# Attention batches on a plan of 25 FFN groups, held outputs of five tiles stored by SyncE, and five more query chunks transposed by DMA

## The chip, the cores and the metric

The kernel runs on 1 core of one Trainium2 chip. The metric is the device time of one execution in microseconds (us). The profile is of one execution and counts its span, some 2 us shorter than that time. A run is called slow here when it is over 1.5% above the fastest of the same kernel. The granted clock is the share of TensorE's full clock that the profile shows as granted (1.000 is full); the DMA share is the time that packets took, as a share of the time of the core's 16 DMA engines (it can exceed 1). PSUM is the memory that matmuls write to, and a PSUM tile has to be emptied before it is used again.

## The reference, cut to what matters

```python
def _attn_ref(q, k, v):                        # (8, 8, 576, 64): batch, heads, rows, head size
    q_p = phi(q, cos_w, sin_w)                 # relu(x)*cos, relu(x)*sin side by side: 128 features
    k_p = phi(k, cos_w, sin_w)
    kv = np.einsum('bhsf,bhsd->bhfd', k_p, v)
    z = np.sum(k_p, axis=2)
    num = np.einsum('bhsf,bhfd->bhsd', q_p, kv)
    den = np.einsum('bhsf,bhf->bhs', q_p, z)[..., None] + 1e-06
    return num / den
def _moe_ref(x, w1, w2, w3, w_out):            # x: the attention output as 4608 rows of 512
    return ((x @ w1) * (x @ w2) @ w3) @ w_out
```

There are 8 batches of attention, each of five chunks of rows, and 9 tiles of 512 rows for the feed-forward part (FFN). Both share TensorE.

Of the kernel before, what the change touches and what calls it, by code (L numbers as in the profile page):

```python
# [10 lines left out]
FP32 = mybir.dt.float32  # L11
# [5 lines left out]
P = 128  # L17
H, S, D = 8, 576, 64
F = 2 * D
NCH = 5  # L20
# [48 lines left out]
def kernel(  # L69
# [128 lines left out]
    def other_loads(behind):  # L198

        seen = sm.tile([P, 1], BF16, name="seen", bufs=1)  # L200
        nc.gpsimd.tensor_copy(out=seen[:], in_=behind)
        nc.gpsimd.dma_start(out=w2b[:, :, ds(512, 256)], in_=w2v[:, :, ds(512, 256)])
        load_w12(768, 256)
        nc.gpsimd.dma_start(out=woutb[:], in_=moe_w_out.rearrange("(c p) m -> p c m", p=P))
        for jp in range(8):
            load_w3(jp)
            if jp == 4:
                load(1, "k")
        load(1, "qv")
        load(2, "kqv")  # L210


    w3Ts = {}
# [22 lines left out]
    def order_of(b):  # L236

        return [0, 1, 2, 3, 4] if b % 2 == 0 else [4, 0, 1, 2, 3]

    def dma_q(b):  # L240

        return order_of(b)[5 if b < 2 else 2 if b == 2 else 0:]

    feat = {}

# [201 lines left out]

    def open_held():
        wst_stack.close()
        held_pool.append(ctx.enter_context(tc.tile_pool(name="held", bufs=8)))  # L450

    def store_held():
        osb, g = held.pop(0)
        store(nc.gpsimd, osb[:, :, :], g, 2)

    def ffn_groups(t):
        x = xT[t]
# [47 lines left out]
        for ms in range(3 if t == NT - 1 else 4):  # L505
            ops = ffn_tile()
            for jc in range(8):
                nc.tensor.matmul(ops[:, :], lhsT=abT[:, jc, ts(ms, 128)], rhs=w34b[:, jc, :],  # L508
                                 start=(jc == 0), stop=(jc == 7))
                if jc == 3:  # L510
                    yield
            if ms % 2 == 0:
                if 1 <= t <= 4:
                    osb = held_pool[0].tile([P, 2, 512], FP32, name="held")
                else:
                    pool = (fsb, held_pool[0])[ms // 2]
                    osb = pool.tile([P, 2, 512], FP32, name="osb", bufs=1)
            nc.scalar.copy(out=osb[:, ms % 2, :], in_=ops[:, :])  # L518
            if t == NT - 1:
                store((nc.sync, nc.scalar)[ms % 2], osb[:, ms % 2:ms % 2 + 1, :], 4 * t + ms, 1)  # L520
            elif ms % 2 == 1 and 1 <= t <= 4:
                held.append((osb, 4 * t + ms - 1))
            elif ms % 2 == 1:
                store(nc.gpsimd, osb[:, :, :], 4 * t + ms - 1, 2)
            yield
        if t == NT - 1:
            for at, n, eng in ((0, 256, nc.scalar), (256, 128, nc.sync), (384, 128, nc.scalar)):
# [10 lines left out]
    def prep_units(b, parts=(prep_k, prep_q, prep_v)):  # L538
        return [(lambda f=f, c=c: f(b, c)) for f in parts for c in order_of(b)]

    def load_piece(b, i, dst, c):

        seen = sm.tile([P, 1], BF16, name="seen", bufs=1)
        nc.gpsimd.tensor_copy(out=seen[0:ROWS[c], :], in_=dst[0:ROWS[c], c, 0, 0:1])  # L544
        load(b, "kqv"[i // 2], i % 2)

    def interleaved(b, pieces=range(5)):

        units = []
        for i, c in enumerate(order_of(b)):  # L550
            units.append(lambda c=c: prep_k(b, c))
            if b + 1 < B:
                units.append(lambda c=c, i=i: load_piece(b + 1, pieces[i], feat[b][0], c))
            units.append(lambda c=c: prep_q(b, c))
            if b + 1 < B and i == NCH - 1 and pieces[i] < 5:
                units.append(lambda c=c: load_piece(b + 1, 5, feat[b][1], c))
            units.append(lambda c=c: prep_v(b, c))
        return units

    def spread(units, first, last, slots):  # L560
        for i, u in enumerate(units):
# [30 lines left out]
    for i in range(2):  # L592
        ps_ffn.append(ctx.enter_context(tc.tile_pool(name=f"ps_ffn{len(ps_ffn)}", bufs=2,
                                                     space=bass.MemoryType.PSUM)))

    for t in range(NT):
        slots = [[] for _ in range(24)]
        if t == 0:
            slots[1].append(lambda: x_tr(0, 1, by_vector=True))
            slots[1].append(lambda: q_tr(0, 3, evac=False)[1]())  # L600
            slots[1].append(lambda: num(0, 2))
            slots[3].append(lambda: num(0, 3))
            slots[3].append(lambda: x_tr(0, 2))
            slots[5].append(lambda: x_tr(0, 3))
            slots[6].append(lambda: prep_q(0, 4))
            slots[11].append(lambda: feature_buffers(1))
            slots[8].append(lambda: q_tr(0, 4))
            slots[10].append(lambda: num(0, 4))
            slots[12].append(lambda: x_tr(0, 4))
            slots[14].append(lambda: w3_tr(0))  # L610
            between = [[] for _ in range(32)]
            later = [[] for _ in range(24)]
            spread(prep_units(1, (prep_k,)), 6, 8, between)
            spread(prep_units(1, (prep_q,)), 10, 12, between)
            spread(prep_units(1, (prep_v,)), 13, 13, between)
            attention_at(1, between, kv=(14, 14, 14, 14, 15), tr=(12, 13, 17, 18, 19),
                         nu=(16, 17, 18, 20, 22), xt=(18, 19, 20, 22, 25))
            later[:8] = between[24:32]
            for jp in range(8):
                for part in range(2):  # L620
                    if part == 0 and jp < 7:
                        slots[15].append(lambda jp=jp: w3_tr(jp + 1))
                    slots[15].append(lambda jp=jp, part=part: w34_mm(jp, part))
                    slots[15] += between[2 * jp + part]
            for g in range(16, 24):
                slots[g] += between[g]
            slots[16].append(open_held)
            slots[16].append(lambda: load(3, "kqv"))
            spread(prep_units(2, (prep_k,)), 20, 23, slots)
        elif t == 1:  # L630
            for g in range(24):
                slots[g] += later[g]
            spread(prep_units(2, (prep_q,)), 0, 4, slots)
            spread(prep_units(2, (prep_v,)), 0, 4, slots)
            attention_at(2, slots, kv=(2, 3, 4, 5, 6), tr=(3, 5, 7, 9, 11),
                         nu=(8, 10, 12, 14, 16), xt=(8, 10, 12, 14, 16))
            slots[4].append(lambda: load_piece(4, 0, feat[2][1], 3))
            spread(interleaved(3, range(1, 6)), 6, 23, slots)
        else:
            if t + 1 < B:  # L640
                attention_at(t + 1, slots, kv=(0, 1, 2, 3, 4), tr=(2, 4, 7, 10, 13),
                             nu=(6, 8, 10, 12, 14), xt=(6, 8, 10, 12, 14))
            for g in {5: (3, 9, 15, 20), 6: (1, 6, 11, 16)}.get(t, ()):
                slots[g].append(store_held)
            if t + 2 < B:
                spread(interleaved(t + 2), 0, 22, slots)
        for g, _ in enumerate(ffn_groups(t)):
            for u in slots[g]:
                u()
# [30 lines left out]
```

## The kernel before: the parts that the change and the argument touch

One tile of FFN is a sequence of 24 groups of four 512-column matmuls. Attention work ("units") is put behind these groups by hand. For one batch the units are: features of keys and queries (half on ScalarE, half on VectorE), the value copy on GpSimd, the key-value product `kv_chunk`, the query transpose to `qpT`, the numerator `num` with its normalization on VectorE, and the transpose of the result block to `xT`, which the FFN tile reads.

```python
    def load(b, which, part=None):              # GpSimd's DMA; one batch is six pieces
        ...                                     # k, q, v, each in part 0 (320 KB) and part 1 (256 KB); batch 7: 512 and 64 KB
    def prep_q(b, c):
        features(b, feat_of(b)[1], raw[b, "q"], c)          # ScalarE and VectorE
        if c in dma_q(b):                                   # else by TensorE (line 326) and VectorE
            nc.sync.dma_start_transpose(out=att_of(b)["qpT"][:, :, ds(columns_of(b, c), R)],
                                        in_=feat[b][1][:R, c].rearrange("p h f -> p (h f)"))
    def dma_q(b):
        return order_of(b)[5 if b < 2 else 2 if b == 2 else 0:]
    ...
    def load_piece(b, i, dst, c):               # the copy to `seen` holds the load back until dst is there
        seen = sm.tile([P, 1], BF16, name="seen", bufs=1)
        nc.gpsimd.tensor_copy(out=seen[0:ROWS[c], :], in_=dst[0:ROWS[c], c, 0, 0:1])
        load(b, "kqv"[i // 2], i % 2)
    def interleaved(b, pieces=range(5)):        # features of batch b, and between them the loads of b + 1
        ...
```

In the steady state the features of batch t + 2 are computed during tile t, and between them the pieces of batch t + 3 are loaded. GpSimd stores most outputs; those of tiles 1 to 4 are held and leave in tiles 5 and 6.

## Time and profile before

| | before |
|---|---|
| median of the three runs (us) | 251.34 |
| span of the profiled run (us) | 249.5 |
| TensorE busy (us) | 242.9 |
| TensorE's wait for anything between 24 and 240 us | none listed |
| mean granted clock | 1.000 |

The prediction shows the lines that carry this. Two further views are needed. The first is the list of issues of single transfers (queue, count, and the median us from issue to landing):

```profile
qpT<-qp SPq DMA_TRANSPOSE x28, 6.2
xT<-xblk SPq DMA_TRANSPOSE x30, 5.4
```

The second is the order in time (start, duration, engine, line, what, and the idle time before it). Parts of it are shown below.

```profile
99.66 0.68 POOL L130 DMA_DIRECT2D qs<-in_q_dram  x1 [0.33 <-issue]
...
104.20 0.68 POOL L134 DMA_DIRECT2D qs<-in_q_dram  x1 [0.27 <-issue]
...
114.93 0.72 ACT L267 ACTIVATE qp<-qs,sinv 64x512 bf16<-64x512 bf16 x1
```

### The profile page before, as it was taken

Reading aid. Unit: us, or ns where it says so; the run is one execution under the profiler, and the core shown is the slowest. Engines: PE = TensorE matmul, PEld = TensorE weight load, DVE = VectorE, ACT = ScalarE, POOL = GpSimd, SP = SyncE. Lnnn points to the kernel's source line nnn. Section 1 sums busy time; section 2 is a strip of 40 time slices with the busy share of each in tenths; the row PEclk is TensorE's granted clock in tenths of the full one; section 3 lists DMA queues with packets and bytes.
Section 4 is the critical chain, followed back from the end, with each engine's and each line's share of the span. In section 5 each row is a group of like instructions: output and inputs, shape, how many; then the busy total and the mean of one; then the engine's idle time right before and its main releaser. Section 6 shows DMA issues by size and latency. Waiting matters only on the chain.

```text
span 249.5 us, 4973 instructions
## 1 busy us (share of the span) xinstructions
PE 242.9 (97%) x1879; PEld 130.2 (52%) x1879; DVE 141.6 (57%) x338; ACT 124.5 (50%) x209; POOL 90.9 (36%) x171
## 2 busy tenths in 40 slices
PE   8899999999999999999999999999999999999994
PEld 3478555666555455545545554555455544444443
DVE  7876665657889628905980695189227704312321
ACT  2676325925966656555655555555432242323320
POOL 7754254540533612441433326280365040023000
PEclk9999999999999999999999999999999999999999
DMA  6999999999999999999999989999798992014013
GB/s 191 183 194 199 209 204 205 198 199 198 267 133 172 170 202 158 156 181 125 160 107 206 189 100 191 190 184 159 107 203 254 240 146 65 3 32 137 1 44 127
DMA packets 80760, 39.85 MB, mean 160 GB/s; under 512 B 48224, under 2 KB 77280, under 8 KB 80736
## 3 DMA queue, kind: packets, MB, share of 16 engines
q0 software_dynamic: 37024, 27.20, 72.0%
q1 hardware_dynamic: 43280, 11.87, 31.9%
q10 hardware_dynamic: 432, 0.46, 0.5%
q8 instruction: 15, 0.25, 0.4%
q14 instruction: 9, 0.07, 0.1%
HBM read 38.80 MB, written 9.44 MB: 193 GB/s over the span
## 4 chain that ended last, share of the span: by engine, by line
PE 92%; DMA 3%; DVE 1%; issue 1%; POOL 1%; ACT 0%; POOLq 0%
PE ffnps L462 50%; PE ffnps L508 24%; PE ffnps L230 6%; PE pnum L353 4%; PE pnum L295 4%; DMA qs<-in_q_dram 3%; PE pst L326 2%; PE pst L218 1%; PE pst L390 1%; PE ffnps L531 1%; POOL vs L112 0%; DVE xblk L363 0%; PE pfirst L353 0%; ACT xT L392 0%; DVE qp L263 0%
## 5 line engine op out<-in xcount | busy, mean ns | idle before, releaser
L503 DVE TENSOR_TENSOR abT<-asb,ffnps 128x512 bf16<-128x512 bf16 x68 | 46.5, 683 | 71.4 <-PE ffnps L462 70.6
L462 PE MATMUL ffnps<-xT,w1b 128*128 128x512 bf16 (+2 forms) x320 | 74.9, 357 | 0.4 <-ACT xT L392 0.2
L462 PE MATMUL ffnps<-xT,w2b 128*128 128x512 bf16 (+2 forms) x320 | 74.9, 357 | 0.0
L499 ACT CAST asb<-ffnps 128x512 bf16<-128x512 f32 x68 | 39.8, 586 | 61.6 <-PE ffnps L462 56.0
L508 PE MATMUL ffnps<-w34b,abT 128*128 128x512 bf16 x280 | 63.0, 379 | 0.0
L462 PEld LDWEIGHTS <-w1b 128*128 128x128 bf16 x320 | 29.4, 98 | 29.6 <-issue 0.6
L508 PEld LDWEIGHTS <-abT 128*128 128x128 bf16 x280 | 26.9, 98 | 31.1
L462 PEld LDWEIGHTS <-w2b 128*128 128x128 bf16 x320 | 26.8, 98 | 20.3
L267 ACT ACTIVATE qp<-qs,sinv 128x512 bf16<-128x512 bf16 (+2 forms) x40 | 28.3, 717 | 1.6 <-DMA qs<-in_q_dram 1.6
L363 DVE TENSOR_TENSOR xblk<-pnum,den 128x512 bf16<-128x512 f32 (+1 forms) x39 | 26.9, 691 | 1.4
L436 POOL DMA_DIRECT2D out_dram<-osb x20 | 10.6, 535 | 46.0 <-ACT osb L518 46.0
L287 POOL COPY va<-vs 128x512 bf16<-128x512 bf16 (+1 forms) x30 | 18.4, 624 | 18.7 <-PE pnum L295 8.9
L267 ACT ACTIVATE kp<-ks,sinv 128x512 bf16<-128x512 bf16 (+1 forms) x35 | 24.7, 721 | 0.0
L518 ACT COPY osb<-ffnps 128x512 f32<-128x512 f32 x19 | 11.1, 585 | 21.9 <-PE ffnps L508 21.9
L353 PEld LDWEIGHTS <-qpT 128*128 128x128 bf16 x320 | 15.1, 98 | 8.6 <-DVE qpT L340 0.6
L263 DVE TENSOR_SCALAR qp<-qs,cosv 128x512 bf16<-128x512 bf16 (+1 forms) x40 | 16.5, 418 | 0.7 <-DMA qs<-in_q_dram 0.6
L295 PEld LDWEIGHTS <-kp 128*128 128x128 bf16 x280 | 13.1, 98 | 7.1
L518 ACT COPY held<-ffnps 128x512 f32<-128x512 f32 x16 | 9.4, 586 | 14.3 <-PE ffnps L508 14.3
L353 PE MATMUL pnum<-kvs,qpT 128*128 128x65 bf16 x312 | 16.5, 194 | 0.0
L544 POOL COPY seen<-kp 128x1 bf16<-128x1 bf16 (+1 forms) x20 | 3.8, 188 | 33.9 <-DVE kp L263 26.1
L230 PE MATMUL ffnps<-woutb,w3T 128*128 128x512 bf16 x64 | 15.4, 379 | 0.0
L295 PE MATMUL pnum<-va,kp 128*128 128x65 bf16 x280 | 14.1, 193 | 0.0
(88 smaller groups left out, 195.3 us busy)
## 6 DMA issues: line engine op xcount, KB each, us to landing
out_dram<-held POOLq DMA_DIRECT2D x10, 256.0 KB, 6.3
qs<-in_q_dram POOLq DMA_DIRECT2D x8, 256.0 KB, 7.9
w3b<-in_moe_w_dram POOLq DMA_DIRECT2D x8, 256.0 KB, 12.8
ks<-in_k_dram POOLq DMA_DIRECT2D x6, 320.0 KB, 10.9
qs<-in_q_dram POOLq DMA_DIRECT2D x6, 320.0 KB, 8.6
vs<-in_v_dram POOLq DMA_DIRECT2D x6, 320.0 KB, 9.0
ks<-in_k_dram POOLq DMA_DIRECT2D x6, 256.0 KB, 8.2
vs<-in_v_dram POOLq DMA_DIRECT2D x6, 256.0 KB, 10.9
```

Of the source, the lines that this page charges most:

```text
L230: nc.tensor.matmul(acc[:, :], lhsT=w3T[:, lc, :], rhs=woutb[:, lc, :], start=(lc == 0), stop=(lc == 7))
L263: nc.vector.tensor_scalar(out=dst[:R, c, :, 0:D], in0=src[:R, :, c, :], scalar1=0.0, scalar2=cosv[:R, at:at + 1], op0=ALU.max, op1=ALU.mult)
L267: nc.scalar.activation(out=dst[:R, c, 0:n, D:F], in_=src[:R, 0:n, c, :], func=ACTF.Relu, scale=sinv[:R, at:at + 1], bias=0.0)
L287: eng.tensor_copy(out=feat_of(b)[2][:R, c, :, 0:D], in_=raw[b, "v"][:R, :, c, :])
L295: nc.tensor.matmul(kvt[:, h // 4, ds((h % 4) * 65, 65)], lhsT=kp[:, c, h, :], rhs=va[:, c, h, 0:D + 1], start=(i == 0 and h % 4 == 0), sto ...
L353: nc.tensor.matmul(nt[:, h // 4, ds((h % 4) * 65, 65)], lhsT=qpT[:, h, ds(at, 128)], rhs=kvs[:, h, :], start=True, stop=True)
L363: nc.vector.tensor_tensor(out=xblk[rows], in0=n4[:, :, :, 0:D], in1=den[rows].unsqueeze(3).to_broadcast([R, 2, 4, D]), op=ALU.mult)
L462: nc.tensor.matmul(out, lhsT=w[:, kc, ts(jc, 128)], rhs=x[:, kc, tok], start=(kc == 0), stop=(kc == 3))
L499: nc.scalar.copy(out=asb[:], in_=aT[:, :])
L503: nc.vector.tensor_mul(out=abT[:, jc, :], in0=asb[:], in1=bT[:, :])
L508: nc.tensor.matmul(ops[:, :], lhsT=abT[:, jc, ts(ms, 128)], rhs=w34b[:, jc, :], start=(jc == 0), stop=(jc == 7))
L518: nc.scalar.copy(out=osb[:, ms % 2, :], in_=ops[:, :])
```

## The change

Its intent: take five more query transposes off TensorE, which is full, and make room on the DMA engines for it. The room is to come from spreading each batch evenly over 25 groups, with one load piece at a time between its steps, and from holding the first outputs until the loads are done. The core of the diff (cuts marked):

```diff
-        return order_of(b)[5 if b < 2 else 2 if b == 2 else 0:]
+        return order_of(b)[5 if b == 0 else 2 if b == 1 else 0:]
...
-        held_pool.append(ctx.enter_context(tc.tile_pool(name="held", bufs=8)))
+        held_pool.append(ctx.enter_context(tc.tile_pool(name="held", bufs=10)))
...
-        store(nc.gpsimd, osb[:, :, :], g, 2)
+        store(nc.sync, osb[:, :, :], g, 2)
...
+    def plan_batch(b):
+        z = 28 + 25 * (b - 2)
+        for i, c in enumerate(order_of(b)):
+            plan[z - 8 + 3 * i // 2].append(lambda c=c: prep_k(b, c))
+            if i == 0 and b > 2:
+                plan[z - 8].append(lambda: behind_k(b, 0, b, "q", 1))
+            plan[z - 5 + i].append(lambda c=c: prep_v(b, c))
+            plan[z - 2 + 2 * i].append(lambda c=c: prep_q(b, c))
+            plan[z + 1 + i].append(lambda c=c, i=i: kv_chunk(b, c, i))
+            plan[z + 8 + 2 * i].append(lambda c=c: num(b, c))
+            if b + 1 < B and i > 0:
+                plan[z + 8 + 2 * i].append(
+                    lambda i=i: behind_x(b, i, b + 1, "kvvq"[i - 1], (1, 0, 1, 0)[i - 1]))
+            plan[z + 8 + 2 * i].append(lambda c=c: x_tr(b, c))
+        if b + 1 < B:
+            plan[z + 7].append(lambda: behind_q(b, 4, b + 1, "k", 0))
...
+    for b in range(2, B):
+        plan_batch(b)
+    for g in (122, 124, 148, 150, *(170 + 5 * i // 2 for i in range(12))):
+        plan[g].append(store_held)
...   (batches 1 and 2 at the start are placed anew in the same manner;
...    `interleaved`, `load_piece` and the stores by GpSimd go)
```

`behind_k`, `behind_q` and `behind_x` copy one element of a key feature, a query feature or a normalized block on GpSimd and then issue the load.

More of the change, by code (lines that the diff above doesn't have):

```diff
@@ L209, in other_loads @@
         load(1, "qv")
-        load(2, "kqv")
     w3Ts = {}
@@ L512, in ffn_groups @@
             if ms % 2 == 0:
-                if 1 <= t <= 4:
-                    osb = held_pool[0].tile([P, 2, 512], FP32, name="held")
-                else:
-                    pool = (fsb, held_pool[0])[ms // 2]
-                    osb = pool.tile([P, 2, 512], FP32, name="osb", bufs=1)
+                osb = held_pool[0].tile([P, 2, 512], FP32, name="held")
             nc.scalar.copy(out=osb[:, ms % 2, :], in_=ops[:, :])
@@ L520, in ffn_groups @@
                 store((nc.sync, nc.scalar)[ms % 2], osb[:, ms % 2:ms % 2 + 1, :], 4 * t + ms, 1)
-            elif ms % 2 == 1 and 1 <= t <= 4:
+            elif ms % 2 == 1:
                 held.append((osb, 4 * t + ms - 1))
-            elif ms % 2 == 1:
-                store(nc.gpsimd, osb[:, :, :], 4 * t + ms - 1, 2)
             yield
@@ L539, in prep_units, with load_behind, behind_k, behind_q @@
         return [(lambda f=f, c=c: f(b, c)) for f in parts for c in order_of(b)]
-    def load_piece(b, i, dst, c):
+    def load_behind(ap, b, name, part):
         seen = sm.tile([P, 1], BF16, name="seen", bufs=1)
-        nc.gpsimd.tensor_copy(out=seen[0:ROWS[c], :], in_=dst[0:ROWS[c], c, 0, 0:1])
-        load(b, "kqv"[i // 2], i % 2)
-    def interleaved(b, pieces=range(5)):
-        units = []
-        for i, c in enumerate(order_of(b)):
-            units.append(lambda c=c: prep_k(b, c))
-            if b + 1 < B:
-                units.append(lambda c=c, i=i: load_piece(b + 1, pieces[i], feat[b][0], c))
-            units.append(lambda c=c: prep_q(b, c))
-            if b + 1 < B and i == NCH - 1 and pieces[i] < 5:
-                units.append(lambda c=c: load_piece(b + 1, 5, feat[b][1], c))
-            units.append(lambda c=c: prep_v(b, c))
-        return units
+        nc.gpsimd.tensor_copy(out=seen[0:64, :], in_=ap)
+        load(b, name, part)
+    def behind_k(b, i, *what):
+        load_behind(feat[b][0][0:64, order_of(b)[i], 0, 0:1], *what)
+    def behind_q(b, i, *what):
+        load_behind(feat[b][1][0:64, order_of(b)[i], 0, 0:1], *what)
+    def behind_x(b, i, *what):
+        c = order_of(b)[i]
+        r = out_rows(b, c).start
+        load_behind(att[b]["x"][c][r:r + 64, 0, 0, 0:1], *what)
+    plan = [[] for _ in range(24 * NT)]
+    def plan_batch(b):
+        z = 28 + 25 * (b - 2)
+        for i, c in enumerate(order_of(b)):
+            plan[z - 8 + 3 * i // 2].append(lambda c=c: prep_k(b, c))
[11 more added lines that the diff above has]
+            plan[z + 7].append(lambda: behind_q(b, 4, b + 1, "k", 0))
     def spread(units, first, last, slots):
@@ L611 @@
             between = [[] for _ in range(32)]
-            later = [[] for _ in range(24)]
             spread(prep_units(1, (prep_k,)), 6, 8, between)
@@ L616 @@
             attention_at(1, between, kv=(14, 14, 14, 14, 15), tr=(12, 13, 17, 18, 19),
-                         nu=(16, 17, 18, 20, 22), xt=(18, 19, 20, 22, 25))
-            later[:8] = between[24:32]
+                         nu=(16, 17, 19, 21, 25), xt=(18, 19, 21, 22, 27))
+            later = between[24:32]
+            for i in range(2):
+                between[11 + i].append(lambda i=i: behind_q(1, 2 + 2 * i, 2, "k", i))
+            between[12].append(lambda: load(2, "v", 0))
+            for i, g in enumerate((16, 17, 19)):
+                between[g].append(lambda i=i: behind_x(1, i, 2, "vqq"[i], (1, 0, 1)[i]))
             for jp in range(8):
@@ L627 @@
             slots[16].append(open_held)
-            slots[16].append(lambda: load(3, "kqv"))
-            spread(prep_units(2, (prep_k,)), 20, 23, slots)
         elif t == 1:
-            for g in range(24):
-                slots[g] += later[g]
-            spread(prep_units(2, (prep_q,)), 0, 4, slots)
-            spread(prep_units(2, (prep_v,)), 0, 4, slots)
-            attention_at(2, slots, kv=(2, 3, 4, 5, 6), tr=(3, 5, 7, 9, 11),
-                         nu=(8, 10, 12, 14, 16), xt=(8, 10, 12, 14, 16))
-            slots[4].append(lambda: load_piece(4, 0, feat[2][1], 3))
-            spread(interleaved(3, range(1, 6)), 6, 23, slots)
-        else:
-            if t + 1 < B:
-                attention_at(t + 1, slots, kv=(0, 1, 2, 3, 4), tr=(2, 4, 7, 10, 13),
-                             nu=(6, 8, 10, 12, 14), xt=(6, 8, 10, 12, 14))
-            for g in {5: (3, 9, 15, 20), 6: (1, 6, 11, 16)}.get(t, ()):
-                slots[g].append(store_held)
-            if t + 2 < B:
-                spread(interleaved(t + 2), 0, 22, slots)
+            for g, units in enumerate(later):
+                slots[g] += units
+        for g in range(24):
+            slots[g] += plan[24 * t + g]
         for g, _ in enumerate(ffn_groups(t)):
```

## The prediction

> **What bounds the kernel now.** I read the page of the profile first, then the busy time by stages, then the waits of TensorE, then the chain of waits, and last the single transfers. The share of busy time and the row of slices come from the page:
>
> ```profile
> PE 242.9 (97%) x1879; PEld 130.2 (52%) x1879; DVE 141.6 (57%) x338; ACT 124.5 (50%) x209; POOL 90.9 (36%) x171
> PE   8899999999999999999999999999999999999994
> PEclk9999999999999999999999999999999999999999
> DMA  6999999999999999999999989999798992014013
> ```
>
> TensorE is busy in 97% of the span at full granted clock, and the others in 57% or less. The digits do not tell a full engine from one with small gaps, so I asked for the busy time in three stretches (us: TensorE first, then weight loads, VectorE, ScalarE, GpSimd, the clock, the DMA share and GB/s):
>
> ```profile
> 24.00:60.00 36.00, 35.96 (x327) 21.52 (x325) 23.38 (x53) 16.64 (x30) 14.70 (x22) 1.00 1.30 203
> 60.00:200.00 140.00, 140.00 (x1094) 72.86 (x1093) 89.04 (x213) 79.33 (x133) 54.13 (x108) 1.00 1.21 176
> 200.00:244.00 44.00, 44.00 (x206) 19.92 (x205) 11.00 (x16) 14.65 (x25) 6.34 (x12) 1.00 0.27 59
> ```
>
> The reader is to see that from 24 to 244 us TensorE lacks 0.04 us in 220. Asked for the waits of TensorE in that stretch, the profile lists none; over the whole span its longest are 1.2 us at the start and 0.9 us for the first values. Busy matmul time alone can hide a slow pitch, so the chain of waits has to say what one instruction costs. From its list in order of time (start, us, what):
>
> ```profile
> by line: PE ffnps L462 49.9%; PE ffnps L508 24.2%; PE ffnps L230 5.5%; PE pnum L353 4.1%; PE pnum L295 3.6%; DMA qs<-in_q_dram 3.2%; PE pst L326 1.6%; PE pst L218 1.4%; PE pst L390 0.9%; issue 0.8%; PE ffnps L531 0.7%; POOL vs L112 0.4%; DV
> ...
> 48.09 0.45 PE pst L326 x8
> 48.53 0.86 PE ffnps L230 x4
> 49.40 0.45 PE pst L326 x8
> ...
> 69.38 0.86 PE ffnps L462 x4
> 70.25 0.45 PE pst L326 x8
> 70.69 0.26 PE pnum L295 x8
> ```
>
> Four matmuls of 512 columns take 0.86 us (216 ns each), eight of 65 columns 0.26 us, eight transposes of one query chunk 0.45 us (56 ns each), and each piece begins where the one before ended. So every transpose of line 326 lies on the path that sets the end, and VectorE, ScalarE, GpSimd and the transfers do not, as long as they deliver in time. They also deliver with difficulty: the DMA share is over 1 until 200 us.
>
> **What the Trainium skill says.** "TensorE: Matmul & The Clock Gate", section "Wait — 56ns, not 53.3ns?", gives 56 ns as the gap between matmuls of 128 columns; the 0.45 us for eight here agree. Its "Part 4: PE-mode transpose" tells of about 275 ns for one transpose in a kernel; the trace shows 219 ns as the modelled length of one, but a pitch of 56 ns, and the pitch is what is saved. "DMA: Bandwidth & Descriptors", section "Queues, rings and completion order", says that each DMA engine alternates between the queues it has work for, packet by packet: a transpose on SyncE's queue and a load on GpSimd's slow each other. The trace agrees: a transpose of a result block (xT) landed in 2.4 us at 175 us, where nothing else moved, and in 6.3 us at 99 us beside a query load. "Issuing engines are not separate DMA queues" on the same page says that another issuing engine only saves issue time; so I expect nothing of SyncE storing in place of GpSimd, beyond freeing GpSimd.
>
> **The change part by part.**
>
> Five query chunks leave TensorE: three of batch 1 (its last three) and two of batch 2 (its first two). The instruction order of the changed kernel has 80 fewer rows on TensorE, 40 weight loads and 40 transposes, and nothing else less. 5 x 0.45 = 2.23 us, all on the path. Their five copies on VectorE (0.68 us each, 3.4 us) go too, off the path. In exchange there are 33 query transposes by DMA in place of 28. One lands in 3.2 to 11.3 us (median 6.2); its use lies 10 groups later in the plan, of 0.86 us each, plus attention matmuls, some 10 us. That should hide.
>
> The outputs of tiles 0 to 4 are kept (10 buffers), two stores of 512 KB leave at groups 122 and 124, two at 148 and 150, and 12 from 170 to 197, all by SyncE. Before, tile 0 stored at 59 and 64 us, amid loads. That removes 1 MB from a crowded stretch. At the end, 12 x 0.5 MB = 6.3 MB within 28 groups (about 24 us) needs 260 GB/s. From 188 to 190 us the trace shows stores at 0.3 to 0.4 MB in a us, so they are done near group 200, before the last tile's first store at group 209. The last stores, 2 to 2.6 us to landing, are unchanged. Cost on the path: 0.
>
> Batches from 2 on follow a plan of 25 groups. The loads are no longer issued a batch ahead: pieces go out at groups 7, 10, 12, 14, 16 and 17 of the plan for features from group 17 on. The first key piece has 10 groups, the second 7 (some 6.8 us with three num steps of 0.26), the last query piece 6. Pieces landed in 4.2 to 6.9 us where they were alone and in 11 to 12 where three were issued together. A late piece stops ScalarE and VectorE, but TensorE has four PSUM tiles and can run about two groups on, so a delay under some 1.7 us costs nothing. I put 0.2 us on the path for all of it.
>
> The close call is xT. Its transpose must land before the next tile's first matmul, and the plan leaves less room than before. For batch 3 the last block that tile 3 needs is normalized behind group 65, and tile 3 starts at group 72: six groups and three num steps, 6 x 0.864 + 3 x 0.26 = 5.96 us. In the trace before, the xT transpose is issued 1.6 us after such a num step begins (118.46 to 120.08 us). So it has to land within 4.3 us. By the same sum tile 5 leaves 4.6 us, tile 7 4.6 us (no loads are left there), tiles 2, 4 and 6 about 5.2 to 5.5 us. Before, with ten query transposes and loads between them, the median was 5.4 us; where one load piece alone was near I read 3.3, 4.0, 5.2 and 6.3 us. In the plan query transposes no longer lie between the xT ones, and I take 4.5 us: nothing at tiles 2, 4, 6 and 7 most of the time, 0.2 us at tile 3 on this figure, and up to 1 us at tiles 3 and 5 if the load of the same step gets in first. I put 0.4 us for these boundaries. There is no buffer in front of them: what is late here is lost in full.
>
> Sum: 251.34 - 2.23 + 0.2 + 0.4 = 249.7 us.
>
> **The rivals.**
>
> (a) Everything hides: 251.34 - 2.23 = 249.1 us. For it: TensorE waits for nothing in the middle now, although DMA is crowded, and the plan spreads transfers. I can't get below that by more than noise, because no other TensorE row goes.
>
> (b) The wait for xT takes the place of the transposes: if each transpose lands at the 5.4 us of before, tile 3 loses 1.1, tile 5 0.8, tile 2 0.2 us: 2.1 us together, and the time is 251.2, the same as before. For it: the DMA share over 1, and each xT step sends a load piece at the same moment. Against it: the stores and the query transposes have left this stretch.
>
> (c) The loads come late: six pieces, 1.7 MB as written, want 8.6 us of DMA at the 0.2 MB per us of the trace, and with 0.7 MB of xT transposes they fill the 10 groups in which they are issued. If key or query pieces land in 9 us or more for each of six batches, ScalarE stops for 2 to 3 us each time, of which about 1 us reaches TensorE: 255 us. For it: the median key piece took 10.9 us before. Against it: those were issued early, several behind one another. The most exposed is batch 2, whose last query piece is issued behind group 19 of tile 0, near 60 us, and is wanted behind group 26, near 65 us.
>
> (d) SyncE gets too full: a DMA transpose held its queue for 1.2 us in the median and 3.9 at most; ten per batch at 2 us each are 20 us of about 24. The stores sit between the batches, where nothing waits behind them. I expect no loss.
>
> **Range and chances.** The floor is 249.1 us less some noise (the three runs of before span 0.3 us), so 248.9. Above, (b) alone gives 251.2 and a bit of (c) more: 251.8. Faster by over 2% would need 246.3 us, which no part provides: 0.01. Slower by over 2% (256.4) needs (c) in full: 0.04. Within 2%: 0.95.
>
> **What would show it.** In the changed profile, line 326's successor should have 48 transposes on TensorE instead of 88, and TensorE should still be full from 24 to 242 us but for short holes. The waits of TensorE should name a DMA of xT, if anything, at the starts of tiles 3 and 5, for 0 to 1 us. Query transposes should never be named. ScalarE should show waits for loads of keys or queries of up to 1.5 us that do not appear in TensorE's list. The number is wrong if TensorE waits at every tile start, if a feature step stops for over 2 us, or if the last stores queue behind held ones and the end behind the last matmul grows beyond the present 3.6 us.

## The result, and the profile after

The changed kernel took 274.59 us (median of 4 runs, 270.77 to 277.35), against 251.3 us. The ratio is 1.0836 (95% interval 1.0726 to 1.0946): 8.4% slower. Ratios in this document use fast runs alone, so they are not quite the ratios of the medians of all runs. Of the changed kernel two runs are fast, 273.98 and 270.77 us; where another kernel's time is compared with the changed one below, it is with their mean, 272.4 us. The four runs had mean granted clocks of 0.967, 0.967, 0.979 and 0.973; the profiled one (273.98 us) counts as fast. From the page of the changed kernel:

```profile
span 272.1 us, 4904 instructions
PE 250.1 (92%) x1839; PEld 130.1 (48%) x1839; DVE 139.0 (51%) x333; ACT 123.1 (45%) x209; POOL 70.1 (26%) x140
PE   8899999999999899599998899959995699999994
PEclk9999999999999999989999799968999799999999
DMA  8999999995799989998899579975999444888803
```

TensorE has 40 matmuls less, as planned (1839 for 1879), and yet it was busy 7.2 us more, and idle 22.0 us instead of 6.6. The digits show holes about once in a batch, and the granted clock dips at or behind most of them. The row of the DMA share dips too, to 5 and 7 where it was 9, so the DMA engines have idle time now. The waits of TensorE (us in total, times, longest):

```profile
PE ffnps L461 <- ACT asb L498: 8.0, 3, 4.9
PE ffnps L461 <- DVE abT L502: 3.4, 1, 3.4
PE ffnps L461 <- DMA xT<-xblk: 3.3, 2, 2.8
```

The first two rows, 11.4 us, name ScalarE and VectorE, which empty TensorE's PSUM tiles. What these two waited for, first ScalarE in the kernel before, then both in the changed kernel:

```profile
ACT qp L267 <- DMA qs<-in_q_dram: 1.6, 2, 1.5
```

```profile
ACT qp L266 <- DMA qs<-in_q_dram: 22.0, 5, 7.2
DVE qp L262 <- DMA qs<-in_q_dram: 19.0, 6, 6.2
```

The 1.6 us of before are at the start of the kernel (11.5 us) nearly in full. Of ScalarE's 22.0 us, 20.5 are four waits, one each in batches 3, 5, 6 and 7, in order of time:

```profile
93.33 0.72 ACT L266 ACTIVATE qp<-qs,sinv 64x512 bf16<-64x512 bf16 x1 [3.15 <-DMA qs<-in_q_dram]
148.85 0.72 ACT L266 ACTIVATE qp<-qs,sinv 64x512 bf16<-64x512 bf16 x1 [4.64 <-DMA qs<-in_q_dram]
179.02 0.72 ACT L266 ACTIVATE qp<-qs,sinv 128x512 bf16<-128x512 bf16 x1 [5.45 <-DMA qs<-in_q_dram]
211.12 0.72 ACT L266 ACTIVATE qp<-qs,sinv 64x512 bf16<-64x512 bf16 x1 [7.24 <-DMA qs<-in_q_dram]
```

The last one can be followed from engine to engine. First the two query pieces of batch 7 (the first feature reads the second, small one), then TensorE and ScalarE around the hole (matmuls of 128x65 are `kv_chunk`):

```profile
199.88 0.89 POOL L112 DMA_DIRECT2D qs<-in_q_dram  x1 [0.27 <-issue]
...
200.94 0.68 POOL L116 DMA_DIRECT2D qs<-in_q_dram  x1
...
207.66 0.42 PE L294 MATMUL pnum<-va,kp 128*128 128x65 bf16 x8
...
212.36 0.56 ACT L498 CAST asb<-ffnps 128x512 bf16<-128x512 f32 x1
...
212.97 1.56 PE L461 MATMUL ffnps<-xT,w1b 128*128 128x512 bf16 x4 [4.89 <-ACT asb L498]
```

The second piece is issued at 200.94 us. ScalarE would have begun the feature at 203.88 (211.12 less the 7.24 it sat idle), 2.9 us later; the piece lands at 211.1, 10.2 us after its issue. On ScalarE the copy that frees a PSUM tile comes behind the feature in the program, and runs at 212.36. TensorE runs on until its PSUM tiles are used up, and stops for 4.89 us. In windows of 2 us (TensorE busy is the second number; the last three are granted clock, DMA share and GB/s):

```profile
208.00:210.00 2.00, 0.08 (x3) 0.00 (x0) 0.00 (x0) 0.00 (x0) 0.00 (x0) 1.00 0.76 248
210.00:212.00 2.00, 0.00 (x0) 0.00 (x0) 0.61 (x2) 0.88 (x2) 0.00 (x0) 1.00 0.05 5
212.00:214.00 2.00, 1.03 (x4) 0.44 (x4) 0.95 (x2) 2.00 (x5) 0.00 (x0) 0.83 0.34 64
214.00:216.00 2.00, 2.00 (x13) 0.95 (x12) 0.95 (x2) 1.77 (x4) 0.00 (x0) 0.50 0.45 87
216.00:218.00 2.00, 2.00 (x23) 1.21 (x22) 0.95 (x2) 0.09 (x1) 0.00 (x0) 0.82 0.92 177
```

After the hole the clock is at half for some 3.4 us, then full again. So one late load costs twice: the hole itself, and then matmuls at half speed. The windows also show the DMA engines first at 248 GB/s (stores that SyncE issued from 200.55 us on were in flight beside the query pieces) and then at 5 GB/s in the midst of the hole: no load is left after batch 7, and the next query transpose is issued at 211.87, behind the late feature. In the batches before, the gated loads slip as well: the first key piece goes out at 75.34, 101.26, 129.67, 158.44 and 188.60 us, so 26 to 30 us apart, where 25 groups of 0.86 us and ten attention steps of 0.26 us are 24.

The sum closes. Span 272.1 - 249.5 = 22.6 us. Waits of TensorE that were not there before: 8.0 + 3.4 + 3.3, and 0.7 for two short ones at batch 1's normalization, 15.4 us. A mean clock of 0.967 over 272.1 us is 9.0 us of full-speed time not granted, and busy TensorE time says about the same: 250.1 - 242.9 + 2.2 = 9.4 us. Less 2.2 us for the transposes: 15.4 + 9.4 - 2.2 = 22.6 us. (Busy and idle time make up the span in any case; what is checked here is that the clock accounts for the longer busy time.) By the granted clock in windows around them, 1.7, 3.4 and 1.7 us were lost behind the query waits of batches 5, 6 and 7, and 1.7 us behind the wait for xT at 114 us. In this one profile, then, query waits stand for 11.4 + 6.8 = 18.2 us and xT for 3.3 + 1.7 = 5.0 us.

The other expected costs: query transposes landed sooner than before, the xT transposes as before.

```profile
qpT<-qp SPq DMA_TRANSPOSE x33, 3.5
xT<-xblk SPq DMA_TRANSPOSE x30, 5.3
```

### The profile page after: what moved, and what is told of

It is laid out like the page before. It is cut to its first block, busy times and chain, and to the rows that moved or that the text cites. A ratio compares the mean times of both kernels' runs of the same rounds, so it can differ in the third digit from the quotient of the medians.

```text
span 272.1 us, 4904 instructions
## 1 busy us (share of the span) xinstructions
PE 250.1 (92%) x1839; PEld 130.1 (48%) x1839; DVE 139.0 (51%) x333; ACT 123.1 (45%) x209; POOL 70.1 (26%) x140
## 4 chain that ended last, share of the span: by engine, by line
PE 68%; DMA 21%; DVE 4%; issue 3%; ACT 2%; POOL 1%; POOLq 0%; DVEq 0%; ACTq 0%
PE ffnps L461 36%; PE ffnps L507 17%; DMA qs<-in_q_dram 16%; PE ffnps L229 5%; DMA xT<-xblk 5%; PE pnum L352 3%; PE pnum L294 3%; DVE xblk L362 2%; PE pst L217 1%; PE pst L389 1%; PE pst L325 1%; PE ffnps L524 1%; ACT asb L498 1%; ACT kp L266 1%; DVE den L361 1%
## 5 line engine op out<-in xcount | busy, mean ns | idle before, releaser
L461 PE MATMUL ffnps<-xT,w1b 128*128 128x512 bf16 (+2 forms) x320 | 77.9, 368 | 11.9 <-ACT asb L498 8.0
L461 PE MATMUL ffnps<-xT,w2b 128*128 128x512 bf16 (+2 forms) x320 | 79.1, 373 | 3.4 <-DVE abT L502 3.4
L507 PE MATMUL ffnps<-w34b,abT 128*128 128x512 bf16 x280 | 66.1, 379 | 0.0
L461 PEld LDWEIGHTS <-w2b 128*128 128x128 bf16 x320 | 29.6, 100 | 32.2 <-issue 6.8
L513 ACT COPY held<-ffnps 128x512 f32<-128x512 f32 x35 | 20.5, 585 | 49.9 <-PE ffnps L507 49.9
L507 PEld LDWEIGHTS <-abT 128*128 128x128 bf16 x280 | 25.5, 98 | 26.3
L262 DVE TENSOR_SCALAR qp<-qs,cosv 128x512 bf16<-128x512 bf16 (+1 forms) x40 | 13.9, 352 | 19.1 <-DMA qs<-in_q_dram 19.0
L294 PEld LDWEIGHTS <-kp 128*128 128x128 bf16 x280 | 14.4, 104 | 9.5 <-issue 3.5
L360 DVE TENSOR_SCALAR den<-pnum 128x8 f32<-128x8 f32 (+1 forms) x39 | 6.4, 165 | 22.2 <-PE pnum L352 22.2
L229 PE MATMUL ffnps<-woutb,w3T 128*128 128x512 bf16 x64 | 15.4, 379 | 0.0
L537 POOL COPY seen<-xblk 64x1 bf16<-64x1 bf16 x23 | 4.4, 190 | 35.9 <-DVE xblk L362 35.9
## 6 DMA issues: line engine op xcount, KB each, us to landing
w3b<-in_moe_w_dram POOLq DMA_DIRECT2D x8, 256.0 KB, 12.8
```

What stands on the lines that cost most here:

```text
L229: nc.tensor.matmul(acc[:, :], lhsT=w3T[:, lc, :], rhs=woutb[:, lc, :], start=(lc == 0), stop=(lc == 7))
L262: nc.vector.tensor_scalar(out=dst[:R, c, :, 0:D], in0=src[:R, :, c, :], scalar1=0.0, scalar2=cosv[:R, at:at + 1], op0=ALU.max, op1=ALU.mult)
L294: nc.tensor.matmul(kvt[:, h // 4, ds((h % 4) * 65, 65)], lhsT=kp[:, c, h, :], rhs=va[:, c, h, 0:D + 1], start=(i == 0 and h % 4 == 0), sto ...
L461: nc.tensor.matmul(out, lhsT=w[:, kc, ts(jc, 128)], rhs=x[:, kc, tok], start=(kc == 0), stop=(kc == 3))
L507: nc.tensor.matmul(ops[:, :], lhsT=abT[:, jc, ts(ms, 128)], rhs=w34b[:, jc, :], start=(jc == 0), stop=(jc == 7))
L513: nc.scalar.copy(out=osb[:, ms % 2, :], in_=ops[:, :])
```

## The experiments

The theory (L in the expectations): the query pieces of the next batch are issued too late and stop ScalarE, VectorE and then TensorE. Rivals: X, loads and DMA transposes collide, so that xT or qpT is late; Q, the added query transposes; S, the stores through SyncE; V, the sheer volume of transfers. Eleven kernels ran, in three sets, each set on one chip beside the kernel before (its medians: 251.53, 251.31 and 251.62 us).

### All later loads away (wrong result)

```diff
     def load_behind(ap, b, name, part):
+        if b > 2:
+            raw[b, name] = raw[2, name]
+            return
```

> The changed kernel with every load after batch 2 taken away (batches 3 to 7 read batch 2's raw data, so the result is wrong on purpose); plan, DMA transposes and stores stay. Theory L (query pieces of the next batch are issued too late, the query features stop ScalarE and VectorE, TensorE stops, and then runs at half clock for a while): no wait for a load is left, so about 249.1 to 249.8 us with clock 1.00. Rival X (the xT transposes are late at the tile starts whatever the loads do): TensorE still waits 2 to 3 us at some tile starts, over 252 us. Rival S (the stores through SyncE disturb): over 252 us with waits near 169 and 200 us.

Measured: 250.73 us, ratio 0.9967 (0.9947 to 0.9987), clock 0.999 in the profiled run. The waits of TensorE list no xT, no qpT, and no ScalarE or VectorE step in the middle but two, on normalized blocks of batch 1 (0.4 and 0.3 us). Plan, DMA transposes and SyncE's stores are all there, so without loads beside them they cost nothing: neither X nor S can be a cost of the transposes or the stores alone. The time is 0.9 us above the range's upper end of 249.8, of which those two waits explain 0.7. That the whole loss (272.4 - 250.8 = 21.6 us, means of the fast runs) hangs on the loads is shown; whether on their lateness or on what they do to the transposes is not yet.

### Only the query wait away (wrong result)

```diff
-                raw[b, name] = ld.tile([P, H, NCH, D], BF16, name=name + "s")
+                raw[b, name] = (raw[3, "q"] if name == "q" and b > 3 else
+                                ld.tile([P, H, NCH, D], BF16, name=name + "s"))
...
-        features(b, feat_of(b)[1], raw[b, "q"], c)
+        features(b, feat_of(b)[1], raw[min(b, 2), "q"], c)
```

All loads run, but from batch 3 on nobody waits for the query pieces.

> The changed kernel with all its loads at their places, but the query features of batches 3 to 7 read batch 2's queries, so nothing waits for the later query pieces any more (wrong result on purpose; from batch 3 on the query pieces land in one buffer that is not read). The mixture on the DMA engines is that of the changed kernel. Theory L (waiting for query pieces is what costs): no wait of ScalarE or VectorE for query loads; what is left are waits of TensorE for xT of 1 to 3 us at some tile starts: 252 to 258 us. If the collision of loads and transposes on the DMA engines is the larger cost and the query wait only comes first: xT waits take its place, 262 us or more, as in the run with the loads a batch ahead.

Measured: 259.47 us, ratio 1.0295 (1.0258 to 1.0332). In means of the fast runs, 12.8 of the 21.6 us go with the query wait alone (272.4 - 259.6), and 8.8 us remain that went in the run without loads (259.6 - 250.8). The theory's range, 252 to 258, is missed by 1.5 us: the second cost was underrated. Its profile names it:

```profile
PE ffnps L462 <- DMA xT<-xblk: 6.1, 2, 3.1
PE pnum L353 <- DMA qpT<-qp: 1.4, 1, 1.4
```

TensorE waits for xT at the starts of tiles. In the changed kernel that wait was 3.3 us; with the query holes gone, more of it comes to light. The clock of this profile (0.987 over 259.2 us) adds 3.4 us at half speed. L is right for the larger part, X for the rest.

### Query features two groups later

```diff
-            plan[z - 2 + 2 * i].append(lambda c=c: prep_q(b, c))
+            plan[z - 2 + 2 * (b > 2) + 2 * i].append(lambda c=c: prep_q(b, c))
```

> The changed kernel with the query features of batches 3 to 7 two groups later in the plan, nothing else (the gate of the next first key piece goes one feature step earlier so that it stays at its group). A dose of the suspected cost: every query piece gets 2 groups, about 1.8 us, more. Theory L: the waits of ScalarE for query loads (3.2, 4.6, 5.5, 7.2 us in the trace) shrink by 1.5 to 2 us each and the time by 8 to 12 us, half-clock time included: 262 to 267 us. If the query loads are not what stops the kernel: 271 us or more.

Measured: 267.75 us, ratio 1.0542 (1.0477 to 1.0608), only two of the four runs fast (263.16 and 267.05 us). Their mean, 265.1 us, lies in the expected range, and is 7.3 us less than the changed kernel's, a little under the expected 8 to 12. The profiled run is a slow one (269.71 us). ScalarE's waits in it for query loads of batches 5, 6 and 7:

```profile
150.84 0.72 ACT L266 ACTIVATE qp<-qs,sinv 64x512 bf16<-64x512 bf16 x1 [0.48 <-DMA qs<-in_q_dram]
182.68 0.72 ACT L266 ACTIVATE qp<-qs,sinv 128x512 bf16<-128x512 bf16 x1 [2.71 <-DMA qs<-in_q_dram]
210.49 0.72 ACT L266 ACTIVATE qp<-qs,sinv 64x512 bf16<-64x512 bf16 x1 [5.35 <-DMA qs<-in_q_dram]
```

Against 4.64, 5.45 and 7.24 us they shrank by 4.2, 2.7 and 1.9 us, and batch 3's wait of 3.15 us is gone. The dose works in the direction of the theory, and in the time roughly in its size. The single waits shrank by more than the dose in part, because TensorE's wait for xT rose from 3.3 to 8.0 us: where TensorE stands for xT just before a feature, as for 2.7 us at 87 us, the query piece has that much longer to land. So the two waits hide each other, and single ones can't be compared to a microsecond between two profiles.

### All six pieces earlier, beside the query transposes

```diff
-            if b + 1 < B and i > 0:
-                plan[z + 8 + 2 * i].append(
-                    lambda i=i: behind_x(b, i, b + 1, "kvvq"[i - 1], (1, 0, 1, 0)[i - 1]))
+            if b + 1 < B and i in (0, 2, 4):
+                plan[z - 2 + 2 * i].append(
+                    lambda i=i: behind_q(b, i, b + 1, "kkq"[i // 2], (0, 1, 0)[i // 2]))
+            if b + 1 < B and i in (1, 3, 4):
+                plan[z + 8 + 2 * i].append(lambda i=i: behind_x(b, i, b + 1, ...))   # q 1, v 0, v 1
...   (the first key piece and the second query piece go from their old places)
```

> The changed kernel with the same six pieces for each later batch, one every four groups from the query features of the batch before on (12 or more groups ahead of the query features instead of 6 or 7); all else stays. Theory L: no query wait over 1 us on ScalarE, 249.1 to 250.5 us. Rival X: still waits at tile starts, over 255 us. Rival V (it is the volume of transfers in total that is too much for the DMA engines, not the moment of issue): 265 us or more, as in the changed kernel.

Measured: ratio 1.0129 (1.0099 to 1.0158); the three fast runs took 253.87 to 255.66 us, three slow ones 257.92 to 261.71. V falls: the same volume costs 18 us less. The theory's 249.1 to 250.5 is missed too. The query wait is gone from ScalarE, and in its place (profile of a slow run, 261.31 us):

```profile
PE pnum L352 <- DMA qpT<-qp: 4.7, 2, 3.2
```

The query transposes, 3.5 us in the changed kernel, now land in 6.2 us in the median and 12.0 at most, because loads run beside them, and their uses lie only ten groups later. That is X's collision, at another place.

### Same places, one batch earlier; and into the gap between the phases

The first puts each piece where the change has it, but for the batch after the next. The second moves the pieces into the gap between the xT steps and the next query transposes. In both, batch 3's pieces go out behind batch 2's first steps.

```diff
# one batch earlier
-                    lambda i=i: behind_x(b, i, b + 1, "kvvq"[i - 1], (1, 0, 1, 0)[i - 1]))
+                    lambda i=i: behind_x(b, i, b + 2, "kvvq"[i - 1], (1, 0, 1, 0)[i - 1]))
...   (the other two pieces likewise)
# into the gap
+                    lambda i=i: behind_k(b, i, b + 1, "qqvv"[i], i % 2))
+                plan[z + 8 + 2 * i].append(lambda i=i: behind_x(b, i, b + 2, "k", i - 3))   # i = 3, 4
# both
+    for g, (name, part, where, i) in zip((22, 24, 26, 28, 30, 32), ...):   # k, k, q, q, v, v
+        plan[g].append(lambda ...: where(2, i, 3, name, part))
```

> The changed kernel with the load pieces in the same places of the plan (beside the xT steps), but each for the batch after the next, so they are ready 25 groups earlier; batch 3's pieces go out behind batch 2's first steps. The DMA engines see nearly the same mixture at the same moments; only lateness of the loads is taken away. Theory L (lateness of query pieces): no wait for a load on ScalarE over 1 us; about 250 to 253 us, what is left being xT waits of TensorE at tile starts (xT landed in 7 to 9 us beside loads in the changed kernel, the tile starts leave 4.3 to 5.5 us). Rival X (the collision of loads and transposes is itself the cost, lateness of loads a follow-up): 260 us or more, with TensorE waiting for xT at most tile starts.

> The changed kernel with the six pieces of a batch two ahead (one ahead for queries and values) moved from beside the xT steps into the gap between the xT steps of one batch and the query transposes of the next (groups 14 to 21 of the plan). Takes away lateness and most of the collision with xT. Theory L and X together: 249.5 to 251.5 us, no wait of TensorE for xT over 0.5 us. If the query transposes that follow are held up by these loads as in the run with early loads, TensorE waits for qpT and the time is 253 us or more.

Measured: 263.51 us, ratio 1.0492 (1.0459 to 1.0526), and 260.79 us, ratio 1.0325 (1.0282 to 1.0368; two of the six runs slow). Both miss the theory's range. The first lies in X's range, with one wait for xT of 2.5 us and not at most tile starts; the second is the case that its expectation gave for qpT waits, 253 us or more. Neither time separates L from X cleanly: my six pieces for batch 3 fell beside batch 2's query transposes, which then landed in up to 14.1 and 12.5 us, and 5.1 and 3.7 us of TensorE's idle time lie between 76 and 86 us in the two profiles. (In the gap version another 3.1 us lie between 177 and 182 us, where batch 6's query transposes landed in up to 11.4 us beside batch 7's loads.) What they do show: no query wait over 1.5 us on ScalarE is left in either, and in the gap version xT lands in 2.5 us in the median and TensorE never waits for it. And after 90 us, where the first run has nearly the changed kernel's mixture with the lateness alone taken away, TensorE has two waits of over 0.3 us, 3.8 us together; the changed kernel's profile has six, 14.7 us together.

### The stores and the query transposes by themselves

```diff
# the kernel before, stores of the change only
-        held_pool.append(ctx.enter_context(tc.tile_pool(name="held", bufs=8)))
+        held_pool.append(ctx.enter_context(tc.tile_pool(name="held", bufs=10)))
-        store(nc.gpsimd, osb[:, :, :], g, 2)
+        store(nc.sync, osb[:, :, :], g, 2)       # all tiles held; stored at the change's groups
# the kernel before, query chunks only
-        return order_of(b)[5 if b < 2 else 2 if b == 2 else 0:]
+        return order_of(b)[5 if b == 0 else 2 if b == 1 else 0:]
```

> The kernel before with only the stores of the change: outputs of five tiles in ten buffers, stored by SyncE at the same groups as in the changed kernel. Theory L: within 0.5 us of before (251.3). Rival S (SyncE's stores hold up transposes, or crowd the loads): 254 us or more. In this kernel the transposes of the batches still run in the groups of the stores, so this is the harsher test for S.

> The kernel before with only the five more query chunks by DMA. Theory L: the transposes by DMA hide, 40 transposes of 56 ns go from TensorE: 249.1 us. Rival Q (the added DMA transposes are what costs, in a stretch where the DMA share is over 1): slower than before, 252 us or more, with TensorE waiting for qpT between 47 and 75 us.

Stores only: 251.65 us, ratio 1.0006 (0.9989 to 1.0024). As the theory had it: the stores cost nothing beside the loads of the kernel before either. Query chunks only: 256.59 us, ratio 1.0213 (1.0189 to 1.0237). Here Q was right and I was wrong: the five chunks do not hide where the kernel before is crowded. From its profile:

```profile
PE pnum L353 <- DMA qpT<-qp: 4.4, 3, 2.2
```

Idle time of TensorE lies at 56 to 58 and 64 to 68 us, between batch 1's and batch 2's numerators, and the clock falls to 0.59 in the window after the first. In the changed kernel no such wait exists at these places; there the stores and batch 3's loads have left the stretch (which of the two makes the room was not run).

### The first held stores ten groups later

```diff
-    for g in (122, 124, 148, 150, *(170 + 5 * i // 2 for i in range(12))):
+    for g in (132, 134, 158, 160, *(170 + 5 * i // 2 for i in range(12))):
```

> The changed kernel with the first four held stores ten groups later (behind groups 132, 134, 158 and 160 instead of 122, 124, 148 and 150), so that they no longer leave just as the query pieces of batches 6 and 7 are in flight. If these stores lengthen the query landings (8.3 to 10.9 us with them, 7.5 to 8.9 without): the waits of ScalarE for batches 6 and 7 fall from 5.5 and 7.2 us to about 4 us each, and the time by 3 to 6 us. If the stores have no part: within 2 us of the changed kernel.

Measured: 269.46 us, ratio 1.0747 (1.0698 to 1.0797). In means of the fast runs that is 2.4 us less (272.4 - 270.0), and the intervals of the two ratios overlap, so the time does not decide between the two expectations. The landings speak for the first: the query pieces of batches 6 and 7 took 7.0 to 7.3 and 5.7 to 6.0 us, against 8.3 to 8.9 and 10.2 to 10.9 us in the changed kernel, and ScalarE's waits for them fell to 3.17 and 1.91 us (from 5.45 and 7.24). So stores that leave while these pieces are in flight lengthen their landings, as far as two profiles can show it: batch 3's wait was 0.73 us here instead of 3.15, long before the edit has any effect. And four new waits of ScalarE for held buffers came up (up to 5.6 us), and xT waits of 9.6 us in all; the share of the stores is not measured by the time.

### Pieces where there is room

Three pieces behind the key features in the gap, for the batch after; three beside the xT steps; none beside the query transposes; 11 buffers, and the first stores at groups 130, 148, 150.

```diff
+            if b > 2 and b + 1 < B and i in (0, 1, 2):
+                plan[z - 8 + 3 * i // 2].append(
+                    lambda i=i: behind_k(b, i, b + 1, "kkq"[i], (0, 1, 0)[i]))
...
+            if b > 2 and b + 1 < B and i in (0, 2, 3):
+                plan[z + 8 + 2 * i].append(lambda i=i: behind_x(b, i, b + 1, "q vv"[i], (1, 0, 0, 1)[i]))
...   (batch 3 keeps its pieces beside batch 2's steps, queries ahead of values)
```

> The changed kernel with its pieces placed by the room that the DMA engines have, three beside the key features of the batch before (the gap between xT steps and query transposes) and three beside the xT steps, none beside the query transposes, all 10 or more groups ahead of use (batch 3 keeps its pieces beside batch 2's steps, queries ahead of values), 11 buffers instead of 10 and the early stores where no piece is in flight. If lateness and collision are both the cause and this plan has room for both: 249.5 to 251 us and no query wait over 1 us on ScalarE, so better than both kernels. If a pace of 25 groups has no room for loads and transposes together in any order: 253 us or more.

Measured: 253.37 us, ratio 1.0078 (1.0038 to 1.0118), all six runs fast (252.42 to 255.84). Of the changed kernel's 21 us only 2 are left, with the same transfers. (The profiled run is the fastest of the six.) ScalarE never waits over 1.3 us for a query, and one wait of TensorE is left in the middle of the profiled run (252.42 us):

```profile
PE pnum L352 <- DMA qpT<-qp: 1.6, 1, 1.6
```

So the expectation that it beats both is wrong by 2 to 4 us, and with 253.37 us the measurement lies by a hair in the range given for a pace without room.

### The part that pays

The kernel before with the stores of the change, and only batch 2's two chunks by DMA.

```diff
-        return order_of(b)[5 if b < 2 else 2 if b == 2 else 0:]
+        return order_of(b)[5 if b < 2 else 0:]
```

> The kernel before with the stores of the change and only batch 2's two query chunks more by DMA (batch 1's three stay on TensorE). 16 transposes of 56 ns leave TensorE: 250.5 us if the held stores have freed the stretch from 59 to 68 us enough for these two transposes to land in time; 252 us or more with a wait of TensorE for qpT near 65 us if not (in the run with all five chunks such waits were 4.4 us in all).

Measured: 250.43 us, ratio 0.9951 (0.9931 to 0.997); five fast runs of 250.03 to 250.83 us, one slow of 254.38. It beats both kernels, by 0.5% against the kernel before (far under the 2% of a verdict, but its interval leaves out 1), about the 0.9 us that 16 transposes of 56 ns make. The slow run is the profiled one; it has one wait of 2.9 us for xT near 88 us, and the clock at 0.50 in the window behind it. No fast run of this kernel was profiled, and the two chunks without the stores were not run, so that the stores are needed for the gain is not shown.

| kernel | median of the fast runs (us) | ratio to before | what stops TensorE, by its profile |
|---|---|---|---|
| changed | 272.38 (two runs) | 1.0836 | query loads 11.4 us, xT 3.3, half clock 9 |
| query features later | 265.11 (two runs) | 1.0542 | (slow run: xT 8.0, qpT 3.0, query loads less) |
| first stores later | 269.46 | 1.0747 | xT 9.6, held buffers, query loads less |
| one batch earlier | 263.51 | 1.0492 | qpT 5.1, xT 2.5 |
| into the gap | 259.68 | 1.0325 | qpT 7.0 |
| pieces earlier | 254.49 | 1.0129 | (slow run: qpT 4.7) |
| query chunks only | 256.59 | 1.0213 | qpT 4.4 |
| stores only | 251.65 | 1.0006 | as before |
| query wait away | 259.47 | 1.0295 | xT 6.1, qpT 1.4 |
| all later loads away | 250.73 | 0.9967 | 0.7 us at batch 1 |
| room | 253.37 | 1.0078 | qpT 1.6 |
| stores and two chunks | 250.32 | 0.9951 | (slow run: xT 2.9) |

## Why the prediction was wrong

**What bounds the kernel.** Right: TensorE has no slack from 24 to 244 us, so every microsecond of wait is paid in full. The changed kernel pays 15.4 us of them. One sign of being wrong that the prediction itself gave, a feature step that stops for over 2 us, came up four times.

**The transposes, -2.23 us.** Right in size: TensorE has 40 matmuls less. In the run of the kernel before with all five chunks, the step "That should hide" failed, and in the changed kernel it held: query transposes landed in 3.5 us and are not among TensorE's waits.

**The stores, 0.** Right by itself (ratio 1.0006). In the changed kernel stores in flight beside query pieces lengthened two query waits, by the landings in the run with the stores later; the prediction did not consider that.

**The loads, "I put 0.2 us on the path for all of it".** This is the step that failed. It measured 12.8 us for the query pieces alone, which is what goes when only the wait for them goes, with the half clock behind it; the profile of the changed kernel puts 18.2 us on them, of which the longer waits for xT and qpT take some back. Three terms in it were wrong.

1. "The last query piece 6" groups ahead. Groups of the plan are not time from issue to use. The piece is issued only when a step has run, and its copy to `seen` has waited for that step. In batch 7 the gate stands behind the group that ends at 198.78 us, and the piece went out at 200.94, so 2.2 us of the six groups' 5.2 were gone; ScalarE was free at 203.88, when the feature's group ended (203.96), so it was not early. Measured from the issue of the piece that is waited for to the moment ScalarE was free for it, the lead was 4.3 us in batch 3 (85.83 to 93.33 - 3.15), 4.0 in batch 5 (in these two it is the piece with seven groups), 3.5 in batch 6 and 2.9 in batch 7. Measured the same way to the first query feature, the kernel before had 11.0, 15.3, 10.0 and 8.9 us in batches 4 to 7, and these pieces landed in 4.5 to 6.8 us.
2. "Pieces landed in 4.2 to 6.9 us where they were alone." They were not alone. Five pieces go out in 7 to 8 us beside five xT transposes, and the query pieces are last: 7.5, 8.6, 8.9 and 10.2 us to landing. The difference of the two, 3.2 to 7.2 us, is the wait of ScalarE.
3. "A delay under some 1.7 us costs nothing." True as far as it goes: TensorE stopped for 4.89 us where ScalarE was idle for 7.24. But what is above was taken once, where it comes in four of the five batches from 3 to 7.

**A term that was not in the sum at all: the clock.** At or behind each of the four waits of 2.3 to 4.9 us the granted clock was at half for 3.4 us or more. That made 9 of the 22.6 us. Neither the working nor rival (c) had it.

**xT, 0.4 us.** Too small as well, but second. The expected landing was 4.5 us; the median was 5.3 and the largest 9.4. TensorE waited 3.3 us for it in the changed kernel (2.8 of them at the start of tile 3, which the prediction had named) and 6.1 us once the query wait was away. A small reading was wrong beside it: at 175 us, "where nothing else moved", a query transpose issued at 173.8 us was still landing; no load or store moved.

**Rival (c)** named the cause, the engine, and the order of events, and was given 4%. Its argument against itself was that the late key pieces of before "were issued early, several behind one another". That is where the reading went wrong: the 10.9 us to landing of before did not hurt because the key pieces were issued 15 us or more ahead of their use. The change took the lead away and kept the crowding. Its size, 255 us, was too small by the clock and by the length of the waits, and batch 2, which it held to be the most exposed, did not wait.

**What stays open.** How the 8.8 us between the run without the query wait and the run without loads divide between xT, qpT and the clock was not measured by a run, as waits that go make room for others; the one profile without the query wait lists 6.1, 1.4 and 3.4 us. Whether a plan at this pace with all five chunks can be faster than 250.4 us is open: the room version came to 253.4. The new plan without the five chunks, or without the stores, was not run.

## What to carry to other kernels

A load that is gated behind a step has a lead of what is left after the gate, not of the slots in the plan; write down the time of its issue and of its first use, and hold the difference against the landing time in the same crowd, not against the landing of a lone transfer. When one engine both prepares the next batch and empties PSUM, one behind the other in its program, a late load can stop the engine that is the bound, and the gated loads of the batch after slip with it. Take a change of several parts apart before believing its sum: here the stores alone were neutral, two chunks with them gained 0.5%, five chunks without them lost 2%, and the whole change lost 8%.

## What the Trainium skill lacked or had wrong

- "TensorE: Matmul & The Clock Gate", section "HAM oscillation — how this bites in real kernels", gives idle gaps of more than about 3.4 us as what throttles. Here shorter ones were enough: a wait of 2.8 us for xT at 114 us and one of about 2.3 us before 151 us were each followed by half clock. In the gap version waits of up to 2.6 us left the mean clock at 1.000.
- "DMA: Bandwidth & Descriptors", section "Queues, rings and completion order", tells that queues alternate on each engine, but no page has what that does to a transpose's landing beside a load: xT landed in 2.4 us in the median with no loads and in 5.3 us (up to 9.4) beside them; qpT in 3.1 us without and up to 12.0 beside loads issued one every few microseconds.
